# GroupNorm on one core: stores and loads go in runs of four instead of three, and two engines' loops lose their fixed place in instruction memory

## The chip, the cores and the metric

The kernel runs on one core of a Trainium2 chip. The metric is the device time of one execution in microseconds (us), the median of several runs. Names of engines are those of the profile: PE (TensorE), DVE (VectorE), ACT (ScalarE), POOL (GpSimd), SP (SyncE, which here only issues DMAs); a trailing q means that engine's instruction queue.

## The reference

```python
def reference(x, g, b):          # x: 128 x 1024 x 32 x 16 bf16, g and b: 1024 bf16
    G = 32
    xr = x.reshape(B, G, C // G, H, W)
    mu = xr.mean(axis=(2, 3, 4), keepdims=True)
    var = ((xr - mu) ** 2).mean(axis=(2, 3, 4), keepdims=True)
    xn = (xr - mu) / jnp.sqrt(var + 1e-5)
    return xn.reshape(B, C, H, W) * g[None, :, None, None] + b[None, :, None, None]
```

Each of the 128 samples has 32 groups of 32 channels with 512 values each, so a group is 16384 values: one mean, one variance, then one scale and one bias for each channel.

## The kernel before

**Tiles.** A row of SBUF (a partition) holds one group of one sample, 16384 bf16 values. Four samples of 32 groups fill the 128 partitions and make one tile of 4 MB. There are 32 tiles (NT), numbered 0 to 31 here, and six tile buffers xt0 to xt5 (NBUF); tile i uses buffer i mod 6. Each tile is loaded once, normalised in place and stored once. L with three digits, as in L270, is a line of the code in the profile.

**What each engine does to a tile.**
- PE (line 157) waits for the load and sums the tile: 32 matmuls of 512 columns by the identity, all added up in one bank of PSUM.
- DVE (line 176) reduces those 512 columns to minus the mean, in `mean(i)`.
- ACT (line 270) squares the tile with the mean as its bias in two halves, each with a sum, and forms the standard deviation in two small instructions (lines 284 and 291).
- DVE (lines 189, 192, 199) forms the scale and bias of each channel and applies them in 32 instructions, one for each channel of the group (line 209). Its `step(i)` begins with `mean(i + 1)`, so the mean of the next tile stands ahead of the normalisation of this one.

**Loops.** On PE, DVE and ACT the tiles 0 and 1 (HEAD) are written out ahead of a hardware loop of five trips; a trip holds six tiles (2 to 7, 8 to 13, 14 to 19, 20 to 25, 26 to 31). The function `loop` makes it. Its argument `head_slot` fixes the slot of a block of instruction memory at which the loop's first instruction is loaded: slot 0, for all three engines.

**Order of the transfers.** SP's program has no loop: all 64 transfers of 4 MB are written out, and SP issues them in that order from one queue. It stops at each one whose condition doesn't hold: a store waits for DVE's last instruction on its tile, a load waits until the store that used its buffer has landed.

```python
        for i in range(min(NBUF, NT)):
            load(i)
        spacer()
        for i in range(NT):
            j = i % NBUF
            sync.wait_ge(s_dve, i + 1)
            sync.dma_start(out=o_v[i], in_=xt[j][:]).then_inc(st[j], 16)
            if (NT - NBUF - 1 - i) % RUN == 0 and i < NT - NBUF:
                for n in range(max(NBUF, i + 1 + NBUF - RUN), min(i + 1 + NBUF, NT)):
                    load(n)
                spacer()
```

With RUN = 3 the order is: loads 0 to 5; stores 0, 1; loads 6, 7; then eight times three stores and three loads (stores 2 to 4, loads 8 to 10; ... ; stores 23 to 25, loads 29 to 31); then stores 26 to 31. After each run of loads stands a `spacer`, a load of 64 bytes for each partition into a tile that nobody uses, which waits for the spacer before it. There are ten of them.

The functions that the diff touches:

Of the kernel before, what the change touches and what calls it, by code (L numbers as in the profile page):

```python
# [15 lines left out]
EPS = 1e-5  # L16

NBUF = 6
RUN = 3
MM_FREE = 512  # L20
HEAD = 2
SPARE = 32
# [3 lines left out]
def kernel(  # L26
# [62 lines left out]
    def col(t, i):  # L89
        j = i % NBUF  # L90
        return t[:, j : j + 1]

    def loop(engine, step, settle, counts):


        for i in range(HEAD):
            step(i)
        with nc.Fori(
            0,
            TRIPS,  # L100
            1,
            engines=bass.OrderedEngineSet([engine.engine]),
            head_slot={engine.engine: 0},
        ):
            for i in range(HEAD, HEAD + NBUF):
                step(i)
            settle()
            for s, n in counts:
                engine.sem_inc(s, -n)
# [3 lines left out]
    def sync_program(sync):  # L113
# [8 lines left out]
        def load(i):  # L122
            j = i % NBUF
            if i >= NBUF:
                sync.wait_ge(st[j], 16 * (i // NBUF))
            sync.dma_start(out=xt[j][:], in_=x_v[i]).then_inc(ld[j], 16)
# [4 lines left out]
# [9 lines that stand above are left out]
    def tensor_program(pe):  # L140
        pe.wait_ge(s_gb, 32)
        pe.wait_ge(s_rep, 1)
        pe.matmul(  # L143
            out=gb_p[:].rearrange("p a k -> p (a k)"),
            lhsT=rep[:],
            rhs=gb_b[:].rearrange("q a k -> q (a k)"),
            start=True,
            stop=True,
        ).then_inc(s_pe, 1)
        pe.wait_ge(s_eye, 1)  # L150

        def step(i):
            j = i % NBUF
            pe.wait_ge(ld[j], 16)
            pe.sem_inc(ld[j], -16)  # L155
            for k in range(NMM):
                m = pe.matmul(  # L157
                    out=pa[j][:],
                    lhsT=eye[:],
                    rhs=xt[j][:, k * MM_FREE : (k + 1) * MM_FREE],  # L160
                    start=(k == 0),
                    stop=(k == NMM - 1),
                )
            m.then_inc(s_pe, 1)

        loop(pe, step, lambda: None, [])
        pe.drain()
        pe.sem_inc(s_pe, 1)

    def vector_program(dve):  # L170
        dve.memset(ones_b[:], 1.0).then_inc(s_set, 1)  # L171
        dve.tensor_copy(out=gb[:], in_=gb_p[:])._wait_ge(s_pe, 1).then_inc(s_dd, 1)  # L172
        gam, bet = gb[:, 0, :], gb[:, 1, :]

        def mean(i):
            dve.tensor_scalar(  # L176
                out=jd[i % 2][:],
                in0=pa[i % NBUF][:],
                scalar1=-inv_n,
                scalar2=None,  # L180
                op0=ALU.mult,
                op1=ALU.add,
                accum_out=col(negmean, i),
            )._wait_ge(s_pe, i + 2).then_inc(s_mean, 1)

        def step(i):
            j = i % NBUF
            mean(i + 1)
            dve.reciprocal(out=col(rstd, i), in_=col(std, i))._wait_ge(  # L189
                s_std, i + 1  # L190
            ).then_inc(s_dd, 1)
            dve.tensor_scalar(  # L192
                out=scl[j][:],
                in0=gam,
                scalar1=col(rstd, i),
                scalar2=None,
                op0=ALU.mult,
            )._wait_ge(s_dd, 3 * i + 2).then_inc(s_dd, 1)
            dve.scalar_tensor_tensor(  # L199
                out=bia[j][:],  # L200
                in0=scl[j][:],
                scalar=col(negmean, i),
                in1=bet,
                op0=ALU.mult,
                op1=ALU.add,
            )._wait_ge(s_dd, 3 * i + 3).then_inc(s_dd, 1)
            for k in range(KC):
                span = xt[j][:, k * HW : (k + 1) * HW]
                m = dve.tensor_scalar(  # L209
                    out=span,  # L210
                    in0=span,
                    scalar1=scl[j][:, k : k + 1],
                    scalar2=bia[j][:, k : k + 1],
                    op0=ALU.mult,
                    op1=ALU.add,
                )
                if k == 0:
                    m._wait_ge(s_dd, 3 * i + 4)
                if k == KC - 2 and i == HEAD + NBUF - 1:
                    m.then_inc(s_dd, 1)  # L220
            m.then_inc(s_dve, 1)

        def settle():
            dve.wait_ge(s_dd, 3 * (HEAD + NBUF) + 2)

        mean(0)
        loop(
            dve,
            step,
            settle,  # L230
            [(s_pe, NBUF), (s_std, NBUF), (s_dd, 3 * NBUF + 1)],
        )

    def pool_program(pool):
# [26 lines left out]
    def scalar_program(act):  # L261
# [5 lines left out]
        def step(i):  # L267
# [29 lines left out]
            )._wait_ge(s_sq, 3 * i + 3).then_inc(s_std, 1)  # L297

        loop(act, step, lambda: act.drain(), [(s_mean, NBUF), (s_sq, 3 * NBUF)])

    with tc.tile_critical():  # L301
        with nc.Block() as block:
            block.sync(sync_program)
            block.tensor(tensor_program)
            block.vector(vector_program)
            block.gpsimd(pool_program)
            block.scalar(scalar_program)

        nc.sync.wait_ge(s_spare, 16 * spacers[0])
        for j in range(NBUF):  # L310
            nc.sync.wait_ge(st[j], 16 * len(range(j, NT, NBUF)))
# [30 lines left out]
```

## Time and profile before

| | |
|---|---|
| median of 3 runs | 633.87 us (633.05 to 634.19) |
| the profiled execution: its own time | 633.55 us |
| the profiled execution: its span | 631.8 us |
| busy: ACT, DVE, PE | 476.2 us (75%), 375.7 us (59%), 262.4 us (42%) |
| moved by DMA | 268.61 MB, mean 425 GB/s |
| transfers of 4 MB | 32 loads, 32 stores |
| spacers | 10 |

The execution's own time is 1.75 us longer than its span, and the span runs from the first instruction to the last. Busy time is that of an engine's instructions; time spent by its queue in waiting is not in it. The DMA share is an average over the core's 16 DMA engines.

### The profile page before, as it was taken

How to read it: one execution, taken by the hardware profiler on the slowest of the kernel's cores; microseconds unless marked ns; L12 is line 12 of the kernel's file. 1: busy time of each engine (PE TensorE's matmuls, PEld its weight loads, DVE VectorE, ACT ScalarE, POOL GpSimd, SP SyncE). 2: the span in 40 equal slices, each digit the busy share in tenths (PEclk: the TensorE clock that was granted, in tenths of full speed). 3: DMA queues.
4: the chain of work that ended last, by engine and by line, in shares of the span. 5: the costliest groups of instructions: out<-in, count | busy, mean ns of one | idle time of the engine just before them, and what ended most of it. 6: DMA issues, size and time to landing. Idle time of an engine off the chain costs nothing. (4 is left out here: it accounts for less than half of the span.)

```text
span 631.8 us, 3680 instructions
## 1 busy us (share of the span) xinstructions
PE 262.4 (42%) x1025; PEld 106.8 (17%) x1025; DVE 375.7 (59%) x1188; ACT 476.2 (75%) x194; POOL 0.9 (0%) x7
## 2 busy tenths in 40 slices
PE   1987409009602850573077019404730680095000
PEld 0333103003200320231032003101310230032000
DVE  0057477775772677077727745771777177447771
ACT  0496999997994599289919964993899199749930
POOL 0000000000000000000000000000000000000000
PEclk9978858658855985687579559955975786598555
DMA  9999999999999999999999999999999999999986
GB/s 365 430 432 416 434 436 428 434 432 431 428 432 431 432 432 431 434 424 432 432 431 430 438 434 428 436 434 434 428 440 432 434 432 436 431 432 428 432 386 289
DMA packets 10760, 268.61 MB, mean 425 GB/s; under 512 B 2560, under 2 KB 2560, under 8 KB 2560
## 3 DMA queue, kind: packets, MB, share of 16 engines
q1 hardware_dynamic: 10656, 268.52, 99.0%
q8 instruction: 2, 0.03, 0.0%
q14 instruction: 6, 0.05, 0.0%
q10 hardware_dynamic: 96, 0.00, 0.0%
HBM read 134.30 MB, written 134.22 MB: 425 GB/s over the span
## 5 line engine op out<-in xcount | busy, mean ns | idle before, releaser
L270 ACT ACTIVATE ja<-xt,negmean 128x8192 fp8e5<-128x8192 bf16 x64 | 455.5, 7117 | 127.3 <-DVE jd L176 121.3
L157 PE MATMUL pa<-xt,eye 128*128 128x512 bf16 x1024 | 262.2, 421 | 307.4 <-PEq L155 305.2
L209 DVE TENSOR_SCALAR xt<-xt,scl,bia 128x512 bf16<-128x512 bf16 x1024 | 333.7, 407 | 1.2
L157 PEld LDWEIGHTS pa<-xt,eye 128*128 128x128 bf16 x1024 | 106.7, 106 | 462.5 <-issue 369.9
L176 DVE TENSOR_SCALAR_CACHE_REDUCE jd<-pa 128x512 bf16<-128x512 f32 x33 | 22.7, 687 | 143.5 <-PE pa L157 141.8
L189 DVE RECIPROCAL rstd<-std 128x1 f32<-128x1 f32 x32 | 5.2, 162 | 83.7 <-ACT std L291 83.7
L270 ACT ACTIVATION_READ_ACCUMULATOR ja<-xt,negmean 128x1 f32 x64 | 11.9, 186 | 0.0
L291 ACT ACTIVATE std<-sq,half 128x1 f32<-128x1 f32 x32 | 9.4, 295 | 1.0
L284 ACT ACTIVATE half<-sq,eps_t 128x1 f32<-128x1 f32 x32 | 8.9, 278 | 0.0
L199 DVE SCALAR_TENSOR_TENSOR bia<-scl,negmean,gb 128x32 f32<-128x32 f32 x32 | 8.1, 252 | 1.1
L192 DVE TENSOR_SCALAR scl<-gb,rstd 128x32 f32<-128x32 f32 x32 | 7.7, 242 | 1.1
L172 DVE COPY gb<-gb_p 128x64 f32<-128x64 f32 x1 | 0.2, 225 | 10.2 <-PE gb_p L143 10.2
L143 PE MATMUL gb_p<-gb_b,rep 32*128 32x64 bf16 x1 | 0.2, 228 | 11.2 <-DMA gb_b<-in_b_dram 11.2
L176 DVE DVE_READ_ACCUMULATOR jd<-pa 128x1 f32 x33 | 2.7, 83 | 0.0
L265 ACT ACT_TABLE_LOAD x1 | 1.3, 1283 | 1.9 <-issue 1.9
L143 PEld LDWEIGHTS gb_p<-gb_b,rep 32*128 32x128 bf16 x1 | 0.1, 97 | 11.2 <-DMA gb_b<-in_b_dram 11.2
L171 DVE MEMSET ones_b<- 128x128 bf16 x1 | 0.2, 165 | 1.1 <-SPq L301 1.1
L244 POOL TENSOR_SCALAR_AFFINE_SELECT rep<-ones_b 32x128 bf16<-32x128 bf16 x1 | 0.3, 302 | 0.0
L235 POOL TENSOR_SCALAR_AFFINE_SELECT eye<-ones_b 128x128 bf16<-128x128 bf16 x1 | 0.3, 293 | 0.8 <-DVE ones_b L171 0.8
L265 ACT ACTIVATE warm<-eps_t 128x1 f32<-128x1 f32 x1 | 0.2, 203 | 0.0
L253 POOL TENSOR_SCALAR eps_t<-ones_b 128x1 f32<-128x1 bf16 x1 | 0.2, 203 | 0.0
L326 POOL MEMSET const-bfloat16-1.0<- 128x1 bf16 x1 | 0.1, 102 | 0.0
(3 smaller groups left out, 0.3 us busy)
## 6 DMA issues: line engine op xcount, KB each, us to landing
xt<-in_x_dram SPq DMA_DIRECT2D x32, 4096.0 KB, 29.1
out_dram<-xt SPq DMA_DIRECT2D x32, 4096.0 KB, 33.0
spare<-in_x_dram SPq DMA_DIRECT2D x10, 8.0 KB, 29.1
gb_b<-in_g_dram ACTq DMA_DIRECT2D x1, 2.0 KB, 6.5
gb_b<-in_b_dram ACTq DMA_DIRECT2D x1, 2.0 KB, 9.7
```

The lines of the kernel that those rows point to most:

```text
L143: pe.matmul(out=gb_p[:].rearrange("p a k -> p (a k)"), lhsT=rep[:], rhs=gb_b[:].rearrange("q a k -> q (a k)"), start=True, stop=True,).the ...
L157: m = pe.matmul(out=pa[j][:], lhsT=eye[:], rhs=xt[j][:, k * MM_FREE : (k + 1) * MM_FREE], start=(k == 0), stop=(k == NMM - 1),)
L176: dve.tensor_scalar(out=jd[i % 2][:], in0=pa[i % NBUF][:], scalar1=-inv_n, scalar2=None, op0=ALU.mult, op1=ALU.add, accum_out=col(negmean, i),
L189: dve.reciprocal(out=col(rstd, i), in_=col(std, i))._wait_ge(s_std, i + 1).then_inc(s_dd, 1)
L192: dve.tensor_scalar(out=scl[j][:], in0=gam, scalar1=col(rstd, i), scalar2=None, op0=ALU.mult,)._wait_ge(s_dd, 3 * i + 2).then_inc(s_dd, 1)
L199: dve.scalar_tensor_tensor(out=bia[j][:], in0=scl[j][:], scalar=col(negmean, i), in1=bet, op0=ALU.mult, op1=ALU.add,)._wait_ge(s_dd, 3 * i ...
L209: m = dve.tensor_scalar(out=span, in0=span, scalar1=scl[j][:, k : k + 1], scalar2=bia[j][:, k : k + 1], op0=ALU.mult, op1=ALU.add,)
L235: pool.affine_select(out=eye[:], in_=ones_b[:], pattern=[[-1, P]], compare_op=ALU.is_equal, fill=0.0, base=0, channel_multiplier=1,)._wait ...
L265: act.activation(out=warm[:], in_=eps_t[:], func=ACT.Sqrt)
L270: m = act.activation(out=ja[:], in_=xt[j][:, h * F // 2 : (h + 1) * F // 2], func=ACT.Square, bias=col(negmean, i), scale=1.0, accum_out=s ...
L284: act.activation(out=col(half, i), in_=sq[:, 2 * j : 2 * j + 1], func=ACT.Identity, bias=eps_t[:], scale=inv_n,)._wait_ge(s_sq, 3 * i + 1) ...
L291: act.activation(out=col(std, i), in_=sq[:, 2 * j + 1 : 2 * j + 2], func=ACT.Sqrt, bias=col(half, i), scale=inv_n,)._wait_ge(s_sq, 3 * i + ...
```

## The change

`RUN` becomes 4. The order of the transfers is then: loads 0 to 5; stores 0, 1; loads 6, 7; then six times four stores and four loads (stores 2 to 5, loads 8 to 11; ... ; stores 22 to 25, loads 28 to 31); then stores 26 to 31. There are eight spacers. The loops of PE and ACT are made without `head_slot`, so they begin wherever the code ahead of them ends; DVE's loop keeps slot 0.

```diff
-RUN = 3
+RUN = 4
...
-    def loop(engine, step, settle, counts):
+    def loop(engine, step, settle, counts, aligned=False):
...
             engines=bass.OrderedEngineSet([engine.engine]),
-            head_slot={engine.engine: 0},
+            **({"head_slot": {engine.engine: 0}} if aligned else {}),
         ):
...
             settle,
             [(s_pe, NBUF), (s_std, NBUF), (s_dd, 3 * NBUF + 1)],
+            aligned=True,
         )
```

## The prediction

> **What bounds the kernel now.** First the slices of the span on the profile's page: is there an engine or a queue that never rests?
>
> ```profile
> ACT  0496999997994599289919964993899199749930
> DMA  9999999999999999999999999999999999999986
> GB/s 365 430 432 416 434 436 428 434 432 431 428 432 431 432 432 431 434 424 432 432 431 430 438 434 428 436 434 434 428 440 432 434 432 436 431 432 428 432 386 289
> ```
>
> The DMA engines are busy in every slice up to the 38th, at about 432 GB/s, whichever engine computes; ACT, the busiest engine, rests again and again. So up to about 600 us the 64 transfers set the pace, and what ACT does is hidden. Only the last two slices fall off. The windows of that stretch (time, busy time and count of PE, PEld, DVE, ACT and POOL, granted clock, DMA share, GB/s) show where:
>
> ```profile
> 610.00:614.00 4.00, 0.00 (x0) 0.00 (x0) 4.00 (x13) 0.00 (x0) 0.00 (x0) 0.50 0.95 410
> 614.00:616.00 2.00, 0.00 (x0) 0.00 (x0) 2.00 (x8) 0.00 (x0) 0.00 (x0) 0.50 0.31 131
> 616.00:618.00 2.00, 0.00 (x0) 0.00 (x0) 1.69 (x6) 0.00 (x0) 0.00 (x0) 0.50 0.34 147
> 618.00:620.00 2.00, 0.00 (x0) 0.00 (x0) 0.00 (x0) 0.00 (x0) 0.00 (x0) 0.50 1.15 492
> ```
>
> From 614 to 618 us most DMA engines have nothing to do: store 30 is nearly out, and DVE is still normalising tile 31. The chain of waits that ended last says what tile 31 waited for (start, length, what; pieces left out):
>
> ```profile
> 552.48 8.51 PE pa L157 x32
> ...
> 561.75 7.22 ACT ja L270 x2
> ...
> 576.73 7.12 ACT ja L270 x2
> ...
> 591.59 7.12 ACT ja L270 x2
> ...
> 606.16 0.30 ACT std L291
> ...
> 607.25 10.43 DVE xt L209 x32
> ```
>
> It begins at the landing of load 29, the first of the last run of three (552.35 us), and goes through PE, the mean, three tiles of ACT one after the other, and DVE's 32 instructions for tile 31. The timeline of SP's queue shows the issues around it:
>
> ```profile
> 523.37 19.64 SPq L126 DMA_DIRECT2D xt<-in_x_dram  x3
> 543.05 0.43 SPq L120 DMA_DIRECT2D spare<-in_x_dram  x1
> 543.52 74.52 SPq L134 DMA_DIRECT2D out_dram<-xt  x6
> ```
>
> The last of those six stores is issued at 617.71 us and lands at 630.28. So the end has two limits that lie close together: the DMA stream, and the chain from the first load of the last run.
>
> **Runs of four, the tail.** A tile costs ACT more than it costs a run of loads. ACT starts tiles 29, 30 and 31 at 561.75, 576.63 and 591.50: 14.87 us each. Loads that follow one another land every 9.70 us (the trace's landings: 552.35, 562.06). A run of four puts one more tile into the last chain: it starts one load earlier and has one ACT tile more.
>
> Step by step. Number the 64 transfers in queue order. Load 28 becomes number 55 (28 loads and 26 stores go ahead of it). In the profile number 55 is store 25, and it landed at 542.66. From landing to ACT's start, load 29 took 561.75 - 552.35 = 9.40 us (PE 8.51, mean 0.7). So ACT starts tile 28 at 552.06. It is free then: tile 27, whose load is number 50 and landed in a run that began at about 465.2, leaves ACT four tiles after 465.2 + 9.4, at 534. From ACT's start on tile 29 to the issue of store 31 went 617.71 - 561.75 = 55.96 us for three tiles; four take 70.83. Store 31 is issued at 622.9 instead of 617.7, 5.2 us later, which is 14.87 - 9.70.
>
> How much of that shows? The last store took 630.28 - 617.71 = 12.57 us from issue to landing. The trace's DMA packets show why so long: the engines that had idled began its packets at 618.55 and were through by 628.3 to 628.9, and one engine still held packets of store 30, began at 619.85 and ended at 629.93. With store 31 issued at 622.9 no engine is late, so I take 11.4 us (628.8 - 617.71, and 0.35 from last packet to landing). 622.9 + 11.4 = 634.3, against 630.28: 4.0 us of the 5.2 show, and 1.2 are covered by the engine that is late anyway. If that cover weren't there, it would be 5.2. As a bound from the far side, the very first load took 1.00 to 13.52, 12.5 us, with an idle queue: then 5.1.
>
> The Trainium skill has a fit for this term: DMA: Bandwidth & Descriptors, section "Anatomy of one DMA", gives 2.0 us and the bytes by 436 GB/s, fitted on another issuing engine's queue; an estimate from it is 2.0 + 9.6 = 11.6 us, and with it the store would land 0.2 us later than by the row.
>
> **Runs of four, the switches.** The change takes away two of ten turns from loads to stores, with their spacers. What does a turn cost? A spacer is 8 packets of 64 bytes for each DMA engine, 11 ns each in the trace: 0.09 us. More is seen in when loads land. PE starts 0.13 us after each landing, so its timeline shows a run of three:
>
> ```profile
> 142.47 8.70 PE L157 MATMUL pa<-xt,eye 128*128 128x512 bf16 x32 [31.67 <-PEq L155]
> 152.18 7.07 PE L157 MATMUL pa<-xt,eye 128*128 128x512 bf16 x32 [1.02 <-PEq L155]
> 162.82 8.75 PE L157 MATMUL pa<-xt,eye 128*128 128x512 bf16 x32 [3.57 <-PEq L155]
> ```
>
> The second load comes 9.71 us after the first, the third 10.64: the last load of a run, ahead of the turn, loses 0.9. Such losses stand at loads 5, 10, 16 and 25 (1.43, 0.93, 0.97, 0.79), none at the other five turns up to load 29: 4.1 us in nine turns, 2.7 of them in the eight behind load 5. With four-runs, load 28 stands behind the turn at load 5 and six more; at 2.7 / 8 = 0.34 each these cost 2.0, in all 3.45. So load 28 lands about 0.7 us earlier, at 542.0, and all behind it moves along: 4.0 - 0.7 = 3.3 us. Bounds: every turn loses nothing (4.1 earlier), or every turn loses 0.97 (3.1 later). I take the mean of the turns seen.
>
> **Runs of four, the middle.** Here DMA sets the pace, and the change matters only if a store isn't ready when its turn comes. In runs of three, a run of stores holds tiles loaded in the run before. In runs of four it holds two of them and two of the run just loaded; the second of those is the tightest. For tile 25: load 24 is number 47 and lands at 465.2, ACT starts at 474.6, ends tile 25 two tiles later at 504.3, and DVE is through 0.8 + 10.4 us later, at 515.6. SP issues store 25 then, and behind it in SP's queue stand loads 28 to 31. Its place (number 54) comes up at 523.4 on the last DMA engine and some 4.3 us earlier on the first ones, 519. So 3 to 7 us to spare, and the DMA stays fed. Loads 28 to 31 are issued from 516 on and needed from 533 on. Tile 9, in the first such run, has more: DVE done at 203, its place at 211. At the start, store 5 would be issued at 130 (its tile is done at 129.94 in the profile) and is needed at 131. These covers hide the whole of the middle; without them each microsecond of lateness would cost one.
>
> **The loops' place.** One row of ACT's timeline shows a price for entering an aligned loop:
>
> ```profile
> 59.14 7.12 ACT L270 ACTIVATE ja<-xt,negmean 128x8192 fp8e5<-128x8192 bf16 x1 [4.96 <-issue]
> ```
>
> It is the first instruction of ACT's loop (tile 2); the mean was there at 51.1, and ACT still stood for 4.96 us. I expect this to go, and store 5 to be ready at 125. It gains nothing, as DMA sets the pace there. PE shows no such wait at tile 2. Back edges lie ahead of tiles 8, 14, 20 and 26; with three-runs each of these opens a run, and what they cost is hidden in the wait for the load. With four-runs 14 and 26 stand third in a run. If a back edge costs 4.96 us on ACT there, tiles 14, 15 and 26, 27 are late by that, and they are stored only after four more loads. So: 0, and no back edge lies within tiles 28 to 31.
>
> A rule speaks against this part: Runtime: NRT & Kernel Launch, section "Instruction fetch mechanics", says that a taken branch to code outside the two blocks an engine holds stops it for a fetch; the 4.96 us agree with that, and by the rule a loop that lies across blocks could stop at each back edge, which on the places above still adds 0.
>
> **The sum.** Landing of store 31: 542.0 + 9.4 + 70.8 + 11.4 = 633.6. The span ends 1.55 us behind it, as before: 635.2, 3.3 longer than 631.8. The profiled execution's time becomes 633.55 + 3.3 = 636.9. It lies 0.3 under the median of the runs, so the median becomes 637.2.
>
> **Rivals.**
> - *Not slower: the turns give it back.* If longer runs lose nothing at the turns, load 28 lands at 542.66 - 4.1 = 538.6, and the end comes at 630.2: 633.8 us. For it: five turns of nine lost nothing. Against it: two turns fewer of nine should not remove all loss, and the 1.43 us of the first turn is untouched. It decides from load 28 landing before 539.9 (within 0.2% of before). Faster by over 0.2% needs 537.4, which is earlier than 54 loss-free steps of 9.70 behind 13.52.
> - *Stores late in every run.* If the second fresh tile of a run misses its place, the DMA engines run dry in each of the five runs with stores 9, 13, 17, 21 and 25. It begins when a tile takes 7 us more than the rows above give. At 2 us beyond that each: 10 us, 647. PE's slowest tiles (9.8 instead of 8.5 us) take 1.3 of the 7.
> - *A fetch stop in the last chain.* If the unaligned code stops PE or ACT once within tiles 28 to 31, 4.96 us come on top: 642. No branch lies there, and PE's first wait of the run (30 us for load 28) would hide one.
>
> **How the numbers follow.** 0.2% of the time is 1.3 us, about what a measurement of this kernel can tell from no change. My forecast has 0.83, the turns 0.07 (0.05 of it within 0.2%, 0.02 faster), late stores 0.05, a fetch stop 0.05. The range of the likeliest: 2.2 us down (turns, two thirds of the way to their bound) and 2.0 up (turns and the 12.5 us of a first transfer): 635.0 to 639.2. The other cases outside it hold about 0.15.
>
> **What would show it.** Right: the chain of waits begins at load 28's landing near 542 and holds four ACT tiles; store 31 is issued near 622; the DMA engines idle 3 to 5 us ahead of it; ACT's 4.96 us at tile 2 are gone; the middle slices stay at 432 GB/s. Wrong: a chain that begins elsewhere, load 28 before 540, DMA share under 1 between 150 and 600 us, or ACT idle with the releaser "issue" behind tile 28.

## The result, and the profile after

| | before | changed |
|---|---|---|
| median, on one chip | 633.46 us (632.90 to 634.19, 4 runs) | 638.31 us (638.19 to 639.73, 4 runs) |
| the profiled execution: its own time | 633.55 us | 638.19 us |
| the profiled execution: its span | 631.8 us | 636.5 us |

The changed kernel is slower: its time is 1.0082 of the time before, 95% interval 1.0070 to 1.0095. That is 4.85 us by the medians, where 3.3 were forecast; 638.31 lies in the range, 1.1 us above the predicted 637.2. The two profiled executions differ by 4.64 us, and the points below are taken from them.

The slices of the changed kernel show the loss at one place. Up to the 38th, DMA works as before; the last two fall to 294 and 265 GB/s:

```profile
DMA  8999999999999999999999999999999999999966
GB/s 363 430 438 415 427 430 430 443 435 430 430 425 428 437 441 437 425 435 428 428 429 439 435 435 432 423 428 430 428 430 429 435 445 432 428 429 428 430 294 265
```

The windows of the end (time, busy time and count of PE, PEld, DVE, ACT, POOL, clock, DMA share, GB/s):

```profile
614.00:618.00 4.00, 0.00 (x0) 0.00 (x0) 4.00 (x14) 0.00 (x0) 0.00 (x0) 0.50 0.91 393
618.00:620.00 2.00, 0.00 (x0) 0.00 (x0) 2.00 (x8) 0.00 (x0) 0.00 (x0) 0.50 0.08 33
620.00:622.00 2.00, 0.00 (x0) 0.00 (x0) 2.00 (x8) 0.00 (x0) 0.00 (x0) 0.50 0.00 0
622.00:624.00 2.00, 0.00 (x0) 0.00 (x0) 0.92 (x3) 0.00 (x0) 0.00 (x0) 0.50 0.61 262
```

From 620 to 622 us no DMA engine moves anything, while DVE works on tile 31. Before, the DMA share at the worst moment was still 0.31. The chain of waits that ended last begins one load earlier than before and holds four tiles of ACT instead of three (start, length, what):

```profile
542.43 6.32 PE pa L157 x20
...
552.11 7.22 ACT ja L271 x2
...
567.09 7.12 ACT ja L271 x2
...
581.96 7.12 ACT ja L271 x2
...
596.82 7.12 ACT ja L271 x2
...
612.49 10.43 DVE xt L209 x32
```

SP's timeline shows the last run of four loads and the last six stores. The sixth is issued at 622.95 us, 5.24 later than before:

```profile
515.53 17.41 SPq L126 DMA_DIRECT2D xt<-in_x_dram  x4
532.99 0.43 SPq L120 DMA_DIRECT2D spare<-in_x_dram  x1
533.46 89.82 SPq L134 DMA_DIRECT2D out_dram<-xt  x6
```

ACT's wait ahead of tile 2 is gone. Its loop now follows on tile 1 with no gap (52.63 + 0.30 = 52.93, where the last piece of tile 1 overlaps the first of tile 2):

```profile
52.63 0.30 ACT L292 ACTIVATE std<-sq,half 128x1 f32<-128x1 f32 x1
52.83 7.11 ACT L271 ACTIVATE ja<-xt,negmean 128x8192 fp8e5<-128x8192 bf16 x1
```

### The profile page after: what moved, and what is told of

The parts are those of the page before. It is cut to its first block, busy times and chain, and to the rows that moved or that the text cites. A ratio compares the mean times of both kernels' runs of the same rounds, so it can differ in the third digit from the quotient of the medians.

```text
span 636.5 us, 3655 instructions
## 1 busy us (share of the span) xinstructions
PE 257.2 (40%) x1004; PEld 105.9 (17%) x1025; DVE 375.8 (59%) x1188; ACT 476.1 (75%) x194; POOL 0.9 (0%) x7
## 5 line engine op out<-in xcount | busy, mean ns | idle before, releaser
L271 ACT ACTIVATE ja<-xt,negmean 128x8192 fp8e5<-128x8192 bf16 x64 | 455.5, 7117 | 132.6 <-DVE jd L176 130.8
L157 PE MATMUL pa<-xt,eye 128*128 128x512 bf16 x1003 | 257.0, 417 | 310.6 <-PEq L155 306.3
```

What stands on the lines that cost most here:

```text
L157: m = pe.matmul(out=pa[j][:], lhsT=eye[:], rhs=xt[j][:, k * MM_FREE : (k + 1) * MM_FREE], start=(k == 0), stop=(k == NMM - 1),)
L271: m = act.activation(out=ja[:], in_=xt[j][:, h * F // 2 : (h + 1) * F // 2], func=ACT.Square, bias=col(negmean, i), scale=1.0, accum_out=s ...
```

## The experiments

The theory: the loss is the last chain's fourth ACT tile, 14.87 us of ACT against 9.70 us of load, and nothing else. The rivals: the new place of the PE and ACT loops takes part in it; runs of four cost something in the middle or in the stream itself.

**The two parts of the change, one at a time.** First, runs of four with all loops at slot 0:

```diff
 # the kernel before
-RUN = 3
+RUN = 4
```

> Runs of four, all three loops at slot 0 as before. Theory (the last chain holds one ACT tile more; the loops' place is worth nothing): 638.3 us within 0.7, and ACT waits some 5 us at tile 2 again. Rival (part of the loss is the PE and ACT loops' new place): under 637.4, in the extreme 633.5.

638.83 us (638.74 to 639.23, 5 runs); 1.0090 of before (1.0076 to 1.0104). The whole loss is there without the other part. ACT's wait at tile 2 is there too, with no effect (its timeline):

```profile
59.26 7.12 ACT L270 ACTIVATE ja<-xt,negmean 128x8192 fp8e5<-128x8192 bf16 x1 [5.76 <-issue]
```

Then the other part alone:

```diff
 # the changed kernel
-RUN = 4
+RUN = 3
```

> Runs of three, PE's and ACT's loops not fixed. Theory: 633.5 us within 0.7; ACT's 5 us at tile 2 are gone and the time does not move. Rival (the loops' place matters): over 634.7, in the extreme 638.3.

633.93 us (633.28 to 634.21, 11 runs); 1.0009 of before (1.0000 to 1.0018). The loops' place does not make the loss. It gains nothing either, though ACT starts tile 2 at 53.41 us here and at 59.14 in the kernel before. Each of the two runs lies 0.5 us above its counterpart, but with opposite signs for the loops (fixed loops slower with four, free loops slower with three), so these runs show no effect of the loops' place.

This run also shows how close the two limits of the end lie in a run of three. In its profile PE took 9.48 us on tile 29 where the kernel before took 8.51. Store 31 was issued at 618.95 us, 1.24 later than before, and landed 11.8 us after its issue, as the changed kernel's store 31 does with all engines idle (11.79). So in this one execution the chain had just overtaken the stream.

**Only the last run shortened.** The changed kernel, runs of four up to load 27, then two and two:

```diff
 # the changed kernel; store after which a run of loads begins: its first load
-RUN = 4
+ENDS = {1: 6, 5: 8, 9: 12, 13: 16, 17: 20, 21: 24, 23: 28, 25: 30}
...
-            if (NT - NBUF - 1 - i) % RUN == 0 and i < NT - NBUF:
-                for n in range(max(NBUF, i + 1 + NBUF - RUN), min(i + 1 + NBUF, NT)):
+            if i in ENDS:
+                for n in range(ENDS[i], i + 1 + NBUF):
```

> As the changed kernel, but the last eight loads go in runs of 4, 2 and 2 (loads 28, 29 behind store 23, loads 30, 31 behind store 25). Theory (only the last run counts): the last chain begins at load 30, near 562, and holds two ACT tiles; store 31 is issued near 612, ahead of its place, and the DMA stream sets the end: 633.0 to 633.9 us. Rival (runs of four cost in the middle, or the loops' place does): 636 us or more.

633.80 us (632.68 to 634.18, 11 runs); 1.0006 of before (0.9997 to 1.0015). The loss is gone, with five runs of four still in the middle and the loops free. The chain that ended last among the engines begins at load 30 and holds two ACT tiles:

```profile
561.77 9.23 PE pa L157 x32
...
571.76 7.22 ACT ja L271 x2
...
586.74 7.12 ACT ja L271 x2
...
602.40 10.43 DVE xt L209 x32
```

Store 31 is issued at 612.85, and the DMA engines stay fed where the changed kernel's stand idle:

```profile
614.00:618.00 4.00, 0.00 (x0) 0.00 (x0) 0.00 (x0) 0.00 (x0) 0.00 (x0) 0.50 0.98 420
```

It is no faster than the kernel before, although store 31 is issued 4.9 us earlier there than in that one. The stream's own end, with the last landing at 630.45 against 630.28 us, is the limit of both.

**ACT made cheaper than a load.** If the chain loses because a tile costs ACT more than a load costs DMA, runs of four must be free once it costs less. In both runs ACT's second half reads 512 of its 8192 columns, so most of that half is missing from the variance and the result is not the reference's:

```diff
 # the changed kernel, and the same on the kernel before
-                    out=ja[:],
-                    in_=xt[j][:, h * F // 2 : (h + 1) * F // 2],
+                    out=ja[:, 0 : (F // 2 if h == 0 else MM_FREE)],
+                    in_=xt[j][:, h * F // 2 : h * F // 2 + (F // 2 if h == 0 else MM_FREE)],
```

> The changed kernel with ACT's second half of the squares cut from 8192 to 512 columns (that part of the variance is left out), so that a tile costs ACT some 8.2 us, less than a load's 9.70. Theory: the last chain is then shorter than the DMA stream, store 31 is ready near 600 us, and the end is the stream's alone: 632.5 to 633.9 us, and by the two turns saved 0 to 1.4 us (0.7) under the same cut in the kernel before. Rival (runs of four cost in the stream itself): 2 us or more over the same cut in the kernel before.

> The kernel before with the same cut in ACT's second half of the squares (that part of the variance is left out). Theory: the stream sets the end as before, with one late DMA engine: 633.0 to 633.9 us, 0 to 1.4 us over the same cut with runs of four. Rival (the ACT chain still set the end of the kernel before): 632.3 us or less.

Runs of four: 633.09 us (632.97 to 633.91, 11 runs), 0.9997 of before (0.9988 to 1.0006). Runs of three: 633.23 us (633.09 to 633.50, 11 runs), 0.9995 of before (0.9986 to 1.0004). No loss is left: with a cheaper ACT runs of four and three differ by 0.14 us, less than such runs tell apart. And the kernel before gains 0.2 us by the medians (633.43 in the same series), within its interval nothing, from an ACT that saves 6.4 us on each tile (the squares are busy 251.0 us in place of 455.5): its end was the stream's, as the prediction had it. In the run of four the last chain is now DVE's, back to back (a few of its pieces), and it is through at 608.9 us:

```profile
575.09 10.43 DVE xt L209 x32
...
586.80 10.43 DVE xt L209 x32
...
598.51 10.43 DVE xt L209 x32
```

DVE then takes 11.71 us a tile (575.09 to 586.80), still more than a load's 9.70. Runs of four cost nothing all the same, as store 31 is issued at 608.96 us and store 30 lands at 619.87 only. So the two runs show that ACT's time makes the loss; they do not show that the loss ends just where the slowest engine's tile costs less than a load.

**Runs of five.** This was to show both the tail's price for a tile and the cover in the middle, by using it up:

```diff
 # the changed kernel
-RUN = 4
+RUN = 5
```

> As the changed kernel with runs of five (the first run of loads after the first six holds load 6 alone). Theory: the last chain holds five ACT tiles, another 14.87 - 9.70 = 5.2 us. And the middle comes uncovered: stores 10, 15, 20 and 25 hold the fourth fresh tile of a run, ready 9.4 + 4 x 14.87 + 11.2 = 80.1 us after that run's first fresh landing, and their place comes up after eight transfers, 77.6 us; with 0.9 us from issue to data, 3 to 4 us of idle DMA in each of four runs. In all 638.3 + 5.2 + 14 = 657 us (652 to 661). Rival (a fixed slack that a longer run does not use up; only the tail counts): 643.5 us.

669.12 us (one run), against 633.4 for the kernel before on the same chip: slower than the theory's 652 to 661, and far from the rival's 643.5. The middle does come uncovered. The windows ahead of the issue of stores 10 and 15 show a DMA share of 0:

```profile
226.00:230.00 4.00, 0.00 (x0) 0.00 (x0) 3.28 (x11) 4.00 (x1) 0.00 (x0) 0.50 0.00 0
...
329.00:333.00 4.00, 0.00 (x0) 0.00 (x0) 3.33 (x11) 4.00 (x1) 0.00 (x0) 0.50 0.00 0
```

By the landings, stores 10, 15, 20 and 25 come 6.2, 5.2, 5.0 and 4.5 us beyond the usual 9.70, 20.9 us in all where 14 were expected. Two terms were too small. From issue to landing these stores took 12.1 us with an idle queue (229.31 to 241.44 for store 10), and I had counted 0.9 + 9.7 and nothing for the landing beyond what a fed queue shows. And the first tile of the run took 10.5 us from landing to ACT's start in the worst case (147.45 to 157.95), not 9.4. The tail gaps are 8.7 us (stores 30 and 31: 13.26 and 14.86 us) against 4.6 in the changed kernel (store 31: 14.32), so the fifth tile cost 4.1 where 5.2 were expected; 0.7 of the difference goes with a fetch of instructions that falls into the changed kernel's last store and not into this one's (see the tail below). The rest stands at a place that was not thought of. SP's timeline shows it:

```profile
74.75 0.33 SPq L126 DMA_DIRECT2D xt<-in_x_dram  x1
75.12 0.43 SPq L120 DMA_DIRECT2D spare<-in_x_dram  x1
75.60 47.93 SPq L134 DMA_DIRECT2D out_dram<-xt  x5
```

Load 6 alone forms the first run here and must wait until store 0 has landed (74.73 us). Store 1 has been ready since 63.6 but stands behind it in SP's queue. So nothing is queued when store 0 ends, and load 6 and store 1 land 13.25 and 11.18 us after their forerunners: 5.0 us lost. 20.9 + 4.1 + 5.0 is 30.0 of the 30.6 us by which the last landing is later than in the changed kernel. This account was read from the trace after the run; no further run tests it.

**What a turn from loads to stores costs.** The prediction took 0.34 us from the landings. Two kernels with 14 turns instead of ten:

```diff
 # the kernel before with ACT's cut; and the changed kernel, nothing left out
-RUN = 3  /  RUN = 4
+RUN = 2
```

> The kernel before with runs of two (14 turns from loads to stores) and ACT's second half of the squares cut to 512 columns (that part of the variance is left out), so that the DMA stream alone sets the end. If a turn costs 0.34 us, as the prediction took from the landings: 633.2 + 4 x 0.34 = 634.6 us. If the losses come whatever the number of turns: 633.2 us within 0.6.

> The changed kernel with runs of two and nothing left out. Theory: the last chain begins at load 30 and holds two ACT tiles, store 31 is ready near 612 us, the stream sets the end: 633.4 us, or 634.8 if four more turns cost 0.34 us each. Rival (short runs cost more than the tail gives): over 636 us.

With ACT's cut: 634.09 us (633.85 to 634.74, 11 runs), 1.0009 of before (1.0000 to 1.0018); against the same cut with runs of three, on another chip, it is 0.9 us more, 0.2 for a turn. Without the cut: 634.22 us (634.00 to 634.54, 11 runs), 1.0011 of before (1.0002 to 1.0020). That is 0.7 us more than the kernel before, about 0.2 for a turn; but this kernel has free loops, and over runs of three with free loops (633.93) it is 0.3, less than 0.1 for a turn. Both lie between the two values that were set against each other. If a turn has a price, it is smaller than taken: 0.1 to 0.2 us, with the 0.14 us that the two turns fewer of runs of four gave.

Is it the spacer's? The kernel before without spacers:

```diff
 # the kernel before
-        spacer()
...
-                spacer()
...
-        nc.sync.wait_ge(s_spare, 16 * spacers[0])
```

> The kernel before without its ten spacers, runs of three, nothing of the result left out. If the losses at the turns are the spacers': up to 4 us less, 629.5 to 632.5 us. If they are the turn's own, or belong to neither: 632.5 to 633.9 us. If spacers keep stores from disturbing the loads ahead of them: over 634.7 us.

633.86 us (632.49 to 634.47, 11 runs), 1.0002 of before (0.9993 to 1.0011). The spacers are not it: up to 4 us less was expected if they were. In its trace the last load of a run still lands late at the same kind of place (load 5: 11.06 us after its forerunner, load 10: 10.25, load 22: 10.86, load 31: 10.84).

None of these orders beats the kernel before by more than such runs resolve.

## Why the prediction was right, point by point

**The tail** was the cause, and its mechanism held in each step. The terms of the sum, predicted and measured in the profiled execution:

| step | predicted | measured |
|---|---|---|
| landing of load 28 | 542.0 | 542.29 |
| from there to ACT's start on tile 28 | 9.4 us | 9.82 us (to 552.11) |
| from there to the issue of store 31 | 70.8 us | 70.84 us (to 622.95) |
| from issue to landing of store 31 | 11.4 us | 11.79 us (to 634.74) |
| from landing to the end of the span | 1.55 us | 1.73 us (to 636.47) |

The errors, 0.29, 0.42, 0.04, 0.39 and 0.18, have the same sign: the terms add up to 635.15, and the span is 636.47, 1.3 us longer. The first is no more than profiles differ by: load 28 landed at 541.75, 542.29 and 543.11 in the three kernels whose runs of four go on to the end. The second is PE: its 32 matmuls on tile 28 took 8.92 us instead of 8.51.

The fourth, from issue to landing, hides two errors of opposite sign, and its small size is partly luck. The prediction had one DMA engine late with store 30, until 619.85, and the idle ones through with store 31 by 628.9. The packets of the kernel before show five late engines, which end store 30 between 618.66 and 620.25, and eleven that had idled and are through with store 31 by 628.45. So a store that meets idle engines should land after 628.45 - 617.71 + 0.35 = 11.1 us, and in the run of five stores 30 and 31 did, after 11.10 each. The changed kernel's store 31 took 0.7 longer. Its packets show 15 engines ending it between 633.53 and 633.67, and one at 634.27, with a fetch of 8 KB of instructions (309 ns, at 628.97) among that engine's packets. The run with fixed loops shows the same fetch (at 629.75) and the same 11.80; in the run of five the fetch came after the last store had landed. So the cover by the late engines was 0.8 us and not 1.2: 5.24 us later in the issue became 4.46 later in the landing.

The Trainium skill's fit (DMA: Bandwidth & Descriptors, section "Anatomy of one DMA"), which the prediction used for its estimate of 11.6 us, is for another issuing engine's queue. The idle queue's stores took 11.1 to 12.1 us here, on both sides of it. The runs decide.

**The turns.** The price was mis-sized: 0.34 us each, against about 0.2 by the runs of two. Load 28 landed 0.37 us earlier than the transfer in its place before, not 0.7; in the run with fixed loops it was 0.45 later (543.11), so a single profile does not resolve this. Nor are the late landings the turns' alone: in the kernel before, load 2 landed 10.98 us after load 1, 1.28 late, with no turn next to it, and the prediction's count leaves it out. The rival in which the turns give the loss back is refuted: with 14 and with 8 turns the medians lie within a microsecond of that with ten, where the stream sets the end. Its bound for a faster kernel was read too strictly: 54 steps of 9.70 behind 13.52 end at 537.32, just ahead of the 537.4 that was called out of reach.

**The middle** stayed covered. Store 25 was issued at 515.16 (predicted 515.6), store 9 at 203.45 (203), store 5 at 123.65 (125). The DMA slices up to the 38th are full. The rival of late stores did not occur with runs of four, and occurred with five.

**The loops' place** was worth nothing, as stated: the 4.96 us went and the time did not move. A back edge (the jump from the end of a trip to the loop's start) costs far less than the bound of 4.96 us that was weighed for it. In the changed kernel tile 14 stands third in its run, and ACT's timeline shows it uncovered:

```profile
271.07 7.12 ACT L271 ACTIVATE ja<-xt,negmean 128x8192 fp8e5<-128x8192 bf16 x1 [0.40 <-ACTq L300]
```

0.40 us, released by ACT's own queue at the loop's drain. With fixed loops and runs of four ACT has the same two waits, 0.8 us in all. By the Trainium skill (Runtime: NRT & Kernel Launch, section "Instruction fetch mechanics"), a taken branch to code outside the two blocks that an engine holds stops it for a fetch. No such stop shows at these back edges, wherever the loop is placed. At the entry of the fixed loop ACT does stand, for 4.96 and 5.76 us; that it waits there for a fetch is not shown.

## What to carry to other kernels

Where a transfer stream sets the pace, look at what the last batch of loads leaves to the slowest engine: a batch of n loads makes a closing chain of n tiles, and once that chain ends behind the stream, each further tile adds that engine's time less one load's. Batches may be long in the middle, as long as each store is ready at its place, and should be short at the end; short enough is enough, as two and three loads at the end gave the same time here. Work out the store that is ready last in a batch against the place at which its turn comes: with four it had some 7 us to spare here on the last DMA engine (about 3 on the first ones, by the prediction's reading), with five it missed by about 5.

## What the runs showed of the hardware that was not expected

- A store that found the DMA queue idle took 11.1 us (end of the run of five), 11.8 (end of the changed kernel) or 12.1 (middle of the run of five) from issue to landing for 4 MB, where one in a fed stream adds 9.7: an empty queue costs 1.4 to 2.4 us beyond the time in which nothing was queued.
- A fetch of 8 KB of instructions among the packets of the last store goes with one DMA engine that ends 0.6 us behind the others (634.27 against 633.67 at the latest in the changed kernel, 635.05 against 634.46 with fixed loops). The store lands when the last engine is through.
- The 16 DMA engines drift apart in a stream that never pauses. In the kernel before, eleven had ended store 30 at 614.03 to 614.54 us, the last at 620.25. In the changed kernel 14 of 16 were level again by then (618.66 to 618.82; the other two at 619.69 and 619.92), as they had stood waiting for stores.
- Entering a hardware loop that is placed at the start of an instruction block cost ACT 4.96 and 5.76 us; entering the same loop right behind the code ahead of it cost nothing that the trace shows. The other kernels of this case agree: 5.3 to 5.8 us with ACT's loop fixed, no such wait with it free.
